# Finch attention and Fourier mixing on one core: GpSimd ordered behind VectorE's planned port operations, with several forms per chunk and a new order

## Chip, cores and metric

The kernel runs on 1 core of one Trainium2 chip. The metric is device time in microseconds (us) of one execution, and several executions are measured. Engines are named as the profile names them: PE is TensorE, DVE is VectorE, ACT is ScalarE, POOL is GpSimd, SP is SyncE.

## What is computed

```python
state = 0                                   # per batch and head, 48 x 48
for t in range(768):                        # r, k, v, w: 4 batches x 8 heads x 768 x 48
    cur = (u * k_t) outer v_t
    y[t] = r_t @ (state + cur)
    state = w_t[:, None] * state + k_t outer v_t
x = y laid out as (4, 768, 384)
mixed = real(fft(fft(x, axis=1), axis=2))
u = x + mixed
un = (u - mean(u)) / sqrt(var(u) + 1e-6)    # over the 384 columns
out = u + relu(un @ w_ch1) @ w_ch2          # 384 -> 1536 -> 384
```

All inputs and the output are float32; the kernel multiplies on PE mostly in bf16.

## The kernel before

A helper class records operations and a table emits them. `_Prog.op` (lines 168 to 203) notes an operation with the engines that may do it, a planned duration for each, the tiles that it reads and writes, and the operations that it depends on. The table ORDER (lines 40 to 111) was found beforehand: for each of the five engines a list of operation numbers. `_Prog.schedule` (205 to 291) walks the lists with the planned durations, only to hand out the eight PSUM banks. `_Prog.emit` (303 to 395) then writes each engine's instructions in the order of its list, with semaphore waits where an operation depends on another engine's. So an engine takes its instructions strictly in the listed order, and a waiting instruction holds back all that stand behind it on that engine, or in SP's queue.

Some operations are marked as users of the SBUF port that DVE and POOL share (the argument `port`, and every POOL instruction that isn't a DMA). In the plan a marked operation starts only when the other engine's last marked one has ended. Nothing of this is emitted: on the chip no semaphore ties the two.

The work goes over 4 batches of 768 tokens, each in 6 chunks of 128 tokens (24 chunks, numbered n). For a chunk, `load` (288 to 306) brings w, k, r and v, 192 KB each, from seven rotating buffers of each kind, all on SP's queue. `attention` (728 to 883) then does, per chunk:

- the log of w on ACT (742), two matmuls that sum logs over the chunk (744, 748) and exponentials of them (750, 763)
- the bonus: products r*k and r*k*u (767, 769), a reduction per head on DVE (771, `dc`), and `vtd = v*dc` (774)
- `vb`, v in bf16 (777, on ACT or DVE); `rh = r*exp` (782, DVE, out of PSUM); `kh = k*exp` (785, DVE or POOL)
- the transposes of rh and kh: on PE, a bank for each, evicted by ACT or DVE (794 to 808), or for batch 3 (n >= 18) by one DMA on SP's queue (790)
- scores on PE (814), two masked copies on DVE (819), the state's update (844 to 856)
- y on PE (864 to 875), to which the bonus vtd is added: in chunks 0 to 4 of batch 0 by an fp32 matmul with the identity that opens the bank (860), then an eviction (877), elsewhere by DVE's add (879).

`fold` (885 to 913) forms sums and differences of mirrored columns, and from batch 1 on of chunks c and c+3 (`sd`, then `xf`). `mix` (915 to 1058) does the Fourier sums along the sequence (936 to 939) and the columns (963), adds x (968 in batch 0, 979 in the others), takes mean and variance (985), normalises (`un`, 971 or 987), transposes un on PE (998, batches 0 and 1) or by DMA (1004, batches 2 and 3), and goes through the feed-forward: 12 first groups of three matmuls for each half batch (1027), a relu on ACT or DVE (1032), and for each row of 128 tokens three groups of four matmuls (1046), the last add on DVE (1052) and an output DMA on SP's queue (1056). `weights` (713 to 723) brings both weight matrices by three DMAs from POOL's queue, W1 in two halves and W2 in one. 32 matmuls without a use (1101) stand in PE's list as fillers, and 16 at the start (1069).

`mix` of one batch is interleaved with `attention` of the next in all five lists. Helpers record many operations under one line: 537 is every two-input product or sum that DVE or POOL may do, 541 and 542 operations with scalars, 551 and 560 ACT's and 561 DVE's copies.

Of the kernel before, what the change touches and what calls it, by code (L numbers as in the profile page):

```python
# [22 lines left out]
DMA_T, DMA_U, T_RK, T_UN, T_XFER, T_LAT = 18, 2, 1240, 1280, 1500, (1250, 450)  # L23
# [11 lines left out]
YPE = (0, 1, 2, 3, 4)  # L35

# [30 lines left out]
    "act": (  # L67
# [13 lines left out]
    "dve": (  # L81
# [45 lines left out]
class _Op:  # L127
    def __init__(self, alts):
# [10 lines left out]
        self.start = None  # L139
        self.end = None  # L140
        self.inc = False
        self.ready0 = 0


class _Prog:
# [59 lines left out]
    def schedule(self, order):  # L205
# [18 lines left out]
        for left in range(len(self.ops)):  # L224
# [35 lines left out]
            if o.port:  # L260
                port[e] = s + o.dur
# [873 lines left out]
```

## Time and profile before

| | |
|---|---|
| three runs | 193.33, 192.1, 189.92 us; median 192.1 |
| profiled execution | span 188.1 us from the first to the last instruction; its own time is not given beside the span |
| granted TensorE clock | 1.000 |
| DMA | 28.99 MB, 154 GB/s over the span |
| HBM | 23.59 MB read, 4.72 MB written |
| POOL: products rk<-in_r,in_k | 21 of 1033 ns |
| DVE: masked copies (819) | 48 of 678 ns |
| ACT: relu (1035) | 71 of 492 ns |

The table of groups gives for each line, engine and pair of tiles the count, the time busy, the mean of one, and the idle time of the engine just ahead of them with what ended it. Busy times of matmuls overlap, so a busy PE isn't a PE at its peak. In the chain that ended last each piece was released by the one ahead of it; "SPq" there is SP's queue, in which only DMA issues stand. A view of a stretch of time gives for each engine its busy time there, with the number of instructions in brackets.

### The profile page before, as it was taken

Reading aid. Unit: us, or ns where it says so; the run is one execution under the profiler, and the core shown is the slowest. Engines: PE = TensorE matmul, PEld = TensorE weight load, DVE = VectorE, ACT = ScalarE, POOL = GpSimd, SP = SyncE. Lnnn points to the kernel's source line nnn. Section 1 sums busy time; section 2 is a strip of 40 time slices with the busy share of each in tenths; the row PEclk is TensorE's granted clock in tenths of the full one; section 3 lists DMA queues with packets and bytes.
Section 4 is the critical chain, followed back from the end, with each engine's and each line's share of the span. In section 5 each row is a group of like instructions: output and inputs, shape, how many; then the busy total and the mean of one; then the engine's idle time right before and its main releaser. Section 6 shows DMA issues by size and latency. Waiting matters only on the chain.

```text
span 188.1 us, 4561 instructions
## 1 busy us (share of the span) xinstructions
PE 176.4 (94%) x1718; PEld 115.1 (61%) x1718; DVE 161.0 (86%) x359; ACT 125.4 (67%) x297; POOL 107.1 (57%) x127
## 2 busy tenths in 40 slices
PE   5998899589999989999999997999999999999994
PEld 2565576356656657776667664766666666666663
DVE  8899998999997999999999997899999879732233
ACT  2898696469795967799898769884763373447300
POOL 3558899992052927679999887699774200000000
PEclk9999999999999999999999999999999999999999
DMA  6999899999999508989999999977752110630043
GB/s 122 224 203 204 179 204 209 187 200 198 206 182 195 104 0 185 244 171 209 199 216 227 217 140 273 216 142 176 135 97 67 45 42 8 141 105 0 0 167 125
DMA packets 116118, 28.99 MB, mean 154 GB/s; under 512 B 111361, under 2 KB 116098, under 8 KB 116098
## 3 DMA queue, kind: packets, MB, share of 16 engines
q1 hardware_dynamic: 114514, 26.36, 68.0%
q0 software_dynamic: 1584, 2.36, 7.1%
q8 instruction: 13, 0.21, 0.4%
q14 instruction: 7, 0.06, 0.1%
HBM read 23.59 MB, written 4.72 MB: 150 GB/s over the span
## 4 chain that ended last, share of the span: by engine, by line
PE 51%; DVE 19%; POOL 10%; SPq 7%; DMA 5%; issue 4%; ACT 3%; DVEq 0%; ACTq 0%; POOLq 0%
PE bank L1027 19%; PE bank L1046 17%; POOL rk L537 5%; SPq L583 5%; PE bank L963 5%; DVE rkh L537 3%; DMA in_w<-in_w_dram 3%; DVE ah L819 3%; DMA in_k<-in_k_dram 3%; PE bank L939 2%; POOL rkh L537 2%; DVE rkh L782 2%; PE bank L814 2%; DVE rk L537 1%; POOL vtd L537 1%
## 5 line engine op out<-in xcount | busy, mean ns | idle before, releaser
L1027 PE MATMUL bank<-unt,w 128*128 128x384 bf16 x288 | 53.3, 326 | 1.0 <-ACT ht L1035 0.9
L1046 PE MATMUL bank<-w,ht 128*128 128x384 bf16 (+2 forms) x300 | 53.6, 319 | 0.0
L1035 ACT ACTIVATE ht<-bank 128x384 bf16<-128x384 f32 x71 | 32.5, 492 | 14.8 <-PE bank L1027 14.7
L1027 PEld LDWEIGHTS bank<-unt,w 128*128 128x128 bf16 x288 | 26.6, 98 | 17.4 <-ACT ht L1035 1.1
L1046 PEld LDWEIGHTS bank<-w,ht 128*128 128x128 bf16 x300 | 27.6, 97 | 15.6
L819 DVE TENSOR_TENSOR ah<-bank,msk 128x512 bf16<-128x512 f32 x48 | 31.0, 678 | 0.5 <-PE bank L814 0.5
L537 POOL TENSOR_TENSOR rk<-in_r,in_k 128x384 f32<-128x384 f32 x21 | 21.6, 1033 | 9.7 <-DVE dc L771 9.0
L1052 DVE SCALAR_TENSOR_TENSOR osb<-bank,rstd,uf 128x384 f32<-128x384 f32 (+2 forms) x25 | 14.9, 596 | 11.1 <-PE bank L1046 10.6
L537 POOL TENSOR_TENSOR rkh<-in_k,e 128x384 bf16<-128x384 f32 x17 | 17.0, 1002 | 12.1 <-ACT e L763 10.4
L537 POOL TENSOR_TENSOR rk<-rk,ub 128x384 f32<-128x384 f32 x21 | 21.1, 1014 | 2.4 <-DVE rk L537 1.2
L537 POOL TENSOR_TENSOR vtd<-in_v,dc 128x384 f32<-128x384 f32 x22 | 18.7, 856 | 2.7 <-DVE dc L771 1.6
L560 ACT ACTIVATE rkt<-bank 128x512 bf16<-128x512 bf16 x30 | 17.2, 595 | 3.2 <-PE bank L804 1.9
L1033 DVE TENSOR_SCALAR ht<-bank 128x384 bf16<-128x384 f32 x25 | 13.0, 547 | 5.5 <-PE bank L1027 5.5
L537 POOL TENSOR_TENSOR xf<-sd 128x384 bf16<-128x384 f32 (+1 forms) x11 | 11.8, 1084 | 8.0 <-DVE sd L537 7.8
L551 ACT ACTIVATE un<-uf,agg 128x384 bf16<-128x384 f32 x19 | 11.2, 621 | 6.3 <-DVE agg L985 5.3
L551 ACT ACTIVATE lb<-in_w 128x384 bf16<-128x384 f32 x24 | 12.2, 523 | 3.6 <-DMA in_w<-in_w_dram 3.4
L763 ACT ACTIVATE e<-bank 128x392 f32<-128x392 f32 (+1 forms) x24 | 11.7, 496 | 4.0 <-DVE bank L848 1.7
L782 DVE TENSOR_TENSOR rkh<-bank,in_r 128x384 bf16<-128x384 f32 x24 | 13.1, 548 | 0.7 <-ACT bank L750 0.7
L750 ACT ACTIVATE bank<-bank 128x384 f32<-128x384 f32 x24 | 11.6, 488 | 2.5 <-PE bank L744 2.3
L771 DVE TENSOR_REDUCE dc<-rk 128x8 f32<-128x384 f32 x24 | 12.9, 538 | 0.1
L551 ACT ACTIVATE vb<-in_v 128x384 bf16<-128x384 f32 x22 | 11.5, 524 | 0.8 <-DMA in_v<-in_v_dram 0.8
L870 PE MATMUL bank<-vb,ah 128*128 128x48 bf16 x192 | 11.1, 183 | 0.0
(147 smaller groups left out, 353.8 us busy)
## 6 DMA issues: line engine op xcount, KB each, us to landing
in_k<-in_k_dram SPq DMA_DIRECT2D x24, 192.0 KB, 3.7
in_w<-in_w_dram SPq DMA_DIRECT2D x24, 192.0 KB, 3.9
in_v<-in_v_dram SPq DMA_DIRECT2D x24, 192.0 KB, 3.8
in_r<-in_r_dram SPq DMA_DIRECT2D x24, 192.0 KB, 3.9
out_dram<-osb SPq DMA_DIRECT2D x23, 192.0 KB, 2.2
w<-in_moe_w_ch_dram POOLq DMA_DIRECT2D x2, 576.0 KB, 8.5
w<-in_moe_w_ch_dram POOLq DMA_DIRECT2D x1, 1152.0 KB, 15.5
out_dram<-osb SPq DMA_DIRECT2D x1, 128.0 KB, 1.7
```

Source lines behind the costliest of these rows:

```text
L537: return lambda e: e.tensor_tensor(out=o, in0=a, in1=b, op=f)
L551: return lambda e: e.activation(o, a, f, **kw)
L560: {"act": lambda e: e.activation(o(), i(), ACTF.Copy), "dve": lambda e: e.tensor_copy(out=o(), in_=i())}, **kw)
L763: op("act", a_ps(ne), lambda e: e.activation(E2[i2][:, 0:ne], ps(tci)[:, 0:ne], ACTF.Exp), r=[tci], w=[("E2", i2)])
L771: op("dve", v_1(DM), lambda e: e.tensor_reduce(out=dc[:, :], in_=rku[:, :, :], axis=mybir.AxisListType.X, op=ALU.add), r=[("RK", i2)], w=[ ...
L782: op("dve", v_1(DM), lambda e: e.tensor_tensor(out=rh[:, :, 0:D], in0=ps(tce)[:, 0:DM].rearrange("t (h d) -> t h d", d=D), in1=rt[:, :, :] ...
L819: masked[n] = op("dve", v_1(512), lambda e, x=x: e.tensor_tensor(out=ah[:, x:H:2, :], in0=ps(ta[x])[:, :].rearrange("p (h t) -> p h t", t= ...
L1027: ins = e.matmul(ps(t)[:, 0:384], W1[:, m, 256 * (j // 2) + j % 2:256 * (j // 2) + 256:2], unt[:, :, m, :], start=(m == 0), stop=(m == NM ...
L1033: {"dve": lambda e, j=j, t=t, ht=ht: e.tensor_scalar(out=ht[:, j, :], in0=ps(t)[:, 0:384], scalar1=su, scalar2=0.0, op0=ALU.mult, op1=ALU. ...
L1035: "act": lambda e, j=j, t=t, ht=ht: e.activation(ht[:, j, :], ps(t)[:, 0:384], ACTF.Relu, scale=su)},
L1046: ins = e.matmul(ps(t)[:, 0:hi - lo], ht[:, j, 128 * x:128 * x + 128], W2[:, j, lo:hi], start=(j == 0), stop=(j == NJ - 1))
L1052: op("dve", v_1(hi - lo) + 64, lambda e, kb=kb, t=t, o=o, lo=lo, hi=hi: e.scalar_tensor_tensor(out=o[:, lo:hi], in0=ps(t)[:, 0:hi - lo], s ...
```

## The change

Four things are done.

1. POOL waits. In `schedule` each marked POOL operation, its DMAs now included, gets a dependency on the last marked DVE operation that the plan starts ahead of it, so `emit` writes a semaphore wait for it. The plan has DVE wait for POOL as before, and nothing is emitted for that.
2. Forms. A new method `choose` records several ways of doing a step, and the lists name the operations of one of them; the others are dropped. The forms are: rh out of PSUM, or through a row in SBUF (`rh_row`); transposes over two banks, over one bank with one eviction of 1024, or by DMA; the mask in one DVE operation, or as an ACT copy and a product on DVE or POOL; y plus bonus out of PSUM, through a row, or by the fp32 matmul that opens the bank (batch 0); the normalised rows' transposes on PE or by DMA; the adds to u and to the output out of PSUM or through a row. `vb` may also be made on POOL.
3. What the new lists choose. Bonus by fp32 matmul: chunks 1 and 3 of batch 0 (5 chunks before). Transposes: one bank for 8 chunks, two banks for 10, DMA for batch 3's six as before. rh through a row: 2 chunks. Masks in two steps: 4 of 48 (two products on DVE, two on POOL). y through a row: 1 chunk; u through a row: 3 rows. Transposes of un: PE for batch 0 and the first half of batch 1, DMA for the rest (27 on PE against 36, 5 DMAs against 4). `vb`: 17 on ACT, 5 on POOL, 2 on DVE. The fillers stay 32.
4. The lists themselves are new on all five engines. Batches and stages lie much as before. On DVE the last rows of batch 0's feed-forward come in the order kb = 1, 2, 0, 5, 4, 3 (before 1, 0, 2, 5, 4, 3). On SP the first output (kb = 2) still stands behind the load of w for batch 2's chunk 1. The 2 later weight DMAs wait for DVE operations: W1's second half for the last of DVE's products of batch 1 that stand behind batch 0's folds, W2 for the first `un` on DVE. POOL's instructions that wait for DVE are 45 (31 before), DVE's that wait for POOL 44 (35).

```diff
-            alts[e] = (d, fn[e] if isinstance(fn, dict) else fn, (e == "pool" and sem is None) or e in port)
+            alts[e] = (d, fn[e] if isinstance(fn, dict) else fn, e == "pool" or e in port)
...
+    def choose(self, name, *ways):
+        wr0, rd0, left = self.wr, self.rd, []
+        for v, way in enumerate(ways):
+            self.wr = {x: list(y) for x, y in wr0.items()}
+            self.rd = {x: list(y) for x, y in rd0.items()}
+            self.cho = (name, v)
+            way()
+            left.append((self.wr, self.rd))
...
     def schedule(self, order):
+        kept = {o for e in self.ENGS for o in self.order[e]}
+        self.ops = [o for o in self.ops if o in kept]
...
                 if o.port:
-                    p = port["pool" if e == "dve" else "dve"]
-                    late = int(e == "dve" or p <= s)
-                    s = max(s, p)
+                    late = int(e == "dve" or port["dve"] <= s)
+                    s = max(s, port["pool"] if e == "dve" else last.end + self.LAT["pool"] if last else 0)
...
             if o.port:
                 port[e] = s + o.dur
+                if e == "dve":
+                    last = o
+                elif last:
+                    o.deps.add(last)
...
+        def rh_row():
+            op("act", a_ps(DM), lambda e: e.activation(e1[...], ps(tce)[:, 0:DM], ACTF.Exp), ...)
+            vec(DM, tt(rh[:, :, 0:D], rt[:, :, :], e1[:, :, :], ALU.mult), ...)
+        g.choose(("rh", b, c), rh_bank, rh_row)
...
-        op(None, {"act": a_sb(DM), "dve": v_2(DM)},
+        op(None, {"act": a_sb(DM), "dve": v_2(DM), "pool": 560},
...
-        if n >= DMA_T:
+        def tr_one():
+            t = g.tile("a")
+            for x, (rows, name) in enumerate(((rflat, "RH"), (kflat, "KH"))):
...
+            evict(lambda: RKT[i4][:, :, :].rearrange("p h t -> p (h t)"), lambda: psb(t)[:, 0:1024], 1024, 2, ...)
+        g.choose(("tr", b, c), *([tr_two, tr_one, tr_dma] if b else [tr_two, tr_one]))
...
+            def twice(x=x, msk=msk, bk=bk):
+                op("act", a_ps(512), lambda e: e.activation(ah[:, x:H:2, :], ps(bk)[...], ACTF.Copy), ...)
+                masked[n].append(op(None, {"dve": v_2(512), "pool": p_1(512)},
+                                    tt(ah[:, x:H:2, :], ah[:, x:H:2, :], msk, ALU.mult), port=("dve",), ...))
+            g.choose(("mask", b, c, x), once, twice)
...
-        ype = b == 0 and c in YPE
+        g.choose(("x", b, c), add_bank, add_row, *([add_pe] if b == 0 else []))
...
-            if b < DMA_U:
+                g.choose(("un", b, hf), un_pe, un_dma)
```

More of the change, by code (lines that the diff above doesn't have):

```diff
@@ L163, in __init__ @@
         self.count = {}
+        self.cho = None
+    def choose(self, name, *ways):
[6 more added lines that the diff above has]
+            left.append((self.wr, self.rd))
+        self.cho = None
+        self.wr, self.rd = {}, {}
+        for wr, rd in left:
+            for had, has in ((wr, self.wr), (rd, self.rd)):
+                for x, y in had.items():
+                    z = has.setdefault(x, [])
+                    z += [o for o in y if o not in z]
     def tile(self, pool):
@@ L206, in schedule @@
         self.order = {e: [self.ops[int(i)] for i in order[e].split()] for e in self.ENGS}
+        kept = {o for e in self.ENGS for o in self.order[e]}
+        assert all(o in kept or o.cho for o in self.ops)
+        self.ops = [o for o in self.ops if o in kept]
+        for o in self.ops:
+            o.deps &= kept
+            for t in o.tile:
+                t.ops = [x for x in t.ops if x in kept]
         at = {e: 0 for e in self.ENGS}
@@ L209, in schedule @@
         port = {"dve": 0, "pool": 0}
+        last = None
         bank = [None] * 8
@@ L278, in schedule @@
                 o.end = self._land(max(t, s + o.set), o.xfer, sw) + o.post
+                if len(hw) >= 4:
+                    engt[e] = max(engt[e], sum(h[2].end - h[2].post for h in hw[-4:-2]) // 2)
             else:
@@ L472, in bass_rwkv6_finch__then__fnet_fourier_mix_kernel @@
     RSTD = [sb("rstd%d" % i, [NC], FP32) for i in range(2)]
-    UN = [sb("un%d" % i, [3, DM], BF16) for i in range(2 if DMA_U < B else 1)]
+    UN = [sb("un%d" % i, [3, DM], BF16) for i in range(2)]
     UNT = [sb("unt%d" % i, [3, NM, 128], BF16) for i in range(2)]
@@ L818, in attention, with once @@
         for x in range(2):
[L819 to L822 removed]
+            masked[n] = []
+            msk = MSK[:, :].unsqueeze(1).to_broadcast([128, HP, 128])
+            bk = ta[x]
+            def once(x=x, msk=msk, bk=bk):
+                masked[n].append(op("dve", v_1(512), lambda e: e.tensor_tensor(
+                    out=ah[:, x:H:2, :], in0=ps(bk)[:, :].rearrange("p (h t) -> p h t", t=128), in1=msk, op=ALU.mult),
+                    r=[bk, "MSK"], w=[("AH", i2, x)]))
+            def twice(x=x, msk=msk, bk=bk):
+                op("act", a_ps(512), lambda e: e.activation(
+                    ah[:, x:H:2, :], ps(bk)[:, :].rearrange("p (h t) -> p h t", t=128), ACTF.Copy), r=[bk], w=[("AH", i2, x)])
+                masked[n].append(op(None, {"dve": v_2(512), "pool": p_1(512)},
+                                    tt(ah[:, x:H:2, :], ah[:, x:H:2, :], msk, ALU.mult), port=("dve",), r=["MSK"], w=[("AH", i2, x)]))
+            g.choose(("mask", b, c, x), once, twice)
         ty = g.tile("a")
@@ L856, in attention, with ymat @@
                 op("dve", v_1(DM), lambda e: decay(e, s_flat), r=[tds, ("E2", i2)], w=[("ST", c % 2)])
[L858 to L864 removed]
+        def ymat(e, ype=False):
             for q in range(HP):
@@ L872, in ymat, with yop, add_bank, add_row @@
             return ins
-        op("pe", mm(D, 8) + (0 if first else mm(96, 4)), ymat,
-           r=[("AH", i2, 0), ("AH", i2, 1), ("VB", n % 4)]
-           + ([] if first else [("RTB", i4), ("ST", (c + 1) % 2)]), w=[ty])
-        if ype:
-            evict(lambda: xb[:, c, 0:DM], lambda: ps(ty)[:, 0:DM], DM, r=[ty], w=[("X", b % 2, c)])
-        else:
-            op("dve", v_1(DM), lambda e: e.tensor_tensor(
-                out=xb[:, c, 0:DM], in0=ps(ty)[:, 0:DM],
-                in1=vtd[:, :, :].rearrange("t h d -> t (h d)"), op=ALU.add),
-               r=[ty, ("VTD", n % 4)], w=[("X", b % 2, c)])
+        def yop(f):
+            op("pe", mm(D, 8) + (0 if first else mm(96, 4)), f, r=[("AH", i2, 0), ("AH", i2, 1), ("VB", n % 4)]
+               + ([] if first else [("RTB", i4), ("ST", (c + 1) % 2)]), w=[ty])
+        vflat = vtd[:, :, :].rearrange("t h d -> t (h d)")
+        def add_bank():
+            yop(ymat)
+            op("dve", v_1(DM), lambda e: e.tensor_tensor(out=xb[:, c, 0:DM], in0=ps(ty)[:, 0:DM], in1=vflat, op=ALU.add),
+               r=[ty, ("VTD", n % 4)], w=[("X", b % 2, c)])
+        def add_row():
+            yop(ymat)
+            op("act", a_ps(DM), lambda e: e.activation(xb[:, c, 0:DM], ps(ty)[:, 0:DM], ACTF.Copy), r=[ty], w=[("X", b % 2, c)])
+            vec(DM, tt(xb[:, c, 0:DM], xb[:, c, 0:DM], vflat, ALU.add), r=[("VTD", n % 4)], w=[("X", b % 2, c)])
+        def add_pe():
+            op("pe", mm(DM, 4), lambda e: e.matmul(ps(ty)[:, 0:DM], IDF[:, :], vflat, start=True, stop=False, skip_group_check=True),
+               r=["IDF", ("HT", 0, 0), ("VTD", n % 4)], w=[ty])
+            yop(lambda e: ymat(e, True))
+            evict(lambda: xb[:, c, 0:DM], lambda: ps(ty)[:, 0:DM], DM, r=[ty], w=[("X", b % 2, c)])
+        g.choose(("x", b, c), add_bank, add_row, *([add_pe] if b == 0 else []))
         fold(b, c)
```

125 lines of the change are left out of this document (72 added, 53 removed), and 132 rows, old and new, of the table ORDER.

## Prediction

> **What bounds the kernel now.** I read the page's head and its engine shares first, then busy time by stage, then the chain that ended last.
>
> ```profile
> span 188.1 us, 4561 instructions
> ...
> PE 176.4 (94%) x1718; PEld 115.1 (61%) x1718; DVE 161.0 (86%) x359; ACT 125.4 (67%) x297; POOL 107.1 (57%) x127
> ...
> PE 51%; DVE 19%; POOL 10%; SPq 7%; DMA 5%; issue 4%; ACT 3%; DVEq 0%; ACTq 0%; POOLq 0%
> ```
>
> ```profile
> core 0: us, PE busy (x) PEld busy (x) DVE busy (x) ACT busy (x) POOL busy (x), PEclk, DMA share, GB/s
> 0.00:45.00 45.00, 37.82 (x405) 24.20 (x406) 42.21 (x107) 32.19 (x68) 34.13 (x50) 1.00 1.02 193
> 45.00:60.00 15.00, 15.00 (x123) 9.34 (x122) 14.14 (x33) 10.51 (x28) 2.81 (x4) 1.00 1.02 194
> 60.00:70.00 10.00, 9.20 (x114) 6.00 (x113) 9.85 (x18) 8.27 (x22) 6.30 (x7) 1.00 0.37 73
> 70.00:110.00 40.00, 39.91 (x472) 27.78 (x470) 39.55 (x85) 34.49 (x83) 34.58 (x38) 1.00 0.98 206
> 110.00:120.00 10.00, 8.91 (x94) 5.89 (x92) 8.26 (x17) 7.70 (x22) 7.59 (x8) 1.00 1.15 207
> 120.00:158.30 38.30, 38.30 (x346) 24.94 (x345) 34.93 (x79) 22.39 (x56) 21.65 (x24) 1.00 0.47 100
> 158.30:188.20 29.90, 27.30 (x180) 16.96 (x178) 12.02 (x26) 9.85 (x25) 0.00 (x0) 1.00 0.30 86
> ```
>
> Three stages show. Up to 45 us VectorE (DVE) is busy 42.2 of 45 and PE idles 7.2 us: batch 0's attention and folding, paced by DVE. From 45 us PE is busy nearly all the time, except 0.8 us at 60 to 70 and 1.1 us at 110 to 120. After 158.3 only feed-forward matmuls are left, and 2.6 us of run-out. So after 45 us a gain must come out of PE's own work or out of those two holes; before 45 us it must come out of DVE.
>
> The chain, in order of time, says the same:
>
> ```profile
> 39.11 1.27 DVE rkh L537
> ...
> 45.01 2.06 PE bank L1027 x12
> ...
> 55.94 1.30 PE bank L1046 x8
> ...
> 69.79 0.54 DVE osb L1052
> 70.35 0.37 SPq L1056
> ...
> 107.50 5.52 DMA in_w<-in_w_dram
> ...
> 114.50 1.15 PE bank L1027 x6
> ```
>
> The first feed-forward matmul (L1027) starts at 45.0. The hole at 110 to 120 goes back through a late load to SyncE's queue (SPq), which at 70.35 had been released by DVE's third output row.
>
> **The change, part by part.**
>
> *GpSimd (POOL) waits for the DVE operation that the plan puts ahead of it.* These are groups of DVE operations with their shortest, median and longest time (the third, fed from PSUM, never varies), and below them one meeting with POOL in full (POOL first, then DVE):
>
> ```profile
> L537 DVE TENSOR_TENSOR xf<-x x4: 342/1044/1802, 31.5 to 37.5; 128x192 bf16<-128x192 f32 x2, 128x191 bf16<-128x191 f32 x2
> L537 DVE TENSOR_TENSOR rkh<-in_k,e x7: 550/1178/1351, 15.4 to 107.3; 128x384 bf16<-128x384 f32 x7
> L782 DVE TENSOR_TENSOR rkh<-bank,in_r x24: 537/546/558, 10.3 to 136.2; 128x384 bf16<-128x384 f32 x24
> L541 DVE TENSOR_SCALAR ss<-ss,sgs x1: 1383/1383/1383, 7.3 to 7.3; 128x285 bf16<-128x285 bf16 x1
> ```
>
> ```profile
> 33.23 0.61 POOL L537 TENSOR_TENSOR xf<-x 128x191 bf16<-128x191 f32 x1
> 33.77 0.78 POOL L716 DMA_DIRECT2D w<-in_moe_w_ch_dram  x1
> 34.54 0.86 POOL L720 DMA_DIRECT2D w<-in_moe_w_ch_dram  x1
> 35.42 1.00 POOL L537 TENSOR_TENSOR rkh<-in_k,e 128x384 bf16<-128x384 f32 x1
> ```
>
> ```profile
> 33.18 3.47 DVE L537 TENSOR_TENSOR xf<-x 128x192 bf16<-128x192 f32 x2
> ```
>
> Two folds that take 0.34 us each when free took 3.47 us while POOL ran a fold, two weight DMAs and a product without a break: 3.47 - 2 x 0.34 = 2.8 us lost. The products rkh<-in_k,e, 0.55 us when free, lose about 1.18 - 0.55 = 0.6 each; some four of the seven fall before 45 us, 2.2 to 2.5 us. The table mirror ss is single; its free price has no row, between 0.34 (the short folds') and 1.38, so it lost 0 to 1.0, say 0.5. Before 45 us that is 2.8 + 2.2 + 0.5 = 5.5 us on the engine that paces the stage. At 64 us two more meet:
>
> ```profile
> 63.88 1.30 DVE L537 TENSOR_TENSOR rk<-rk,ub 128x384 f32<-128x384 f32 x1
> 65.11 1.18 DVE L537 TENSOR_TENSOR rkh<-in_k,e 128x384 bf16<-128x384 f32 x1
> ```
>
> Another 1.4 us, ahead of the output row at 69.7.
>
> The new waits put DVE's folds (now in one run with the products of batch 1) ahead of POOL's products and of the second weight DMA. In batch 2 DVE is given no marked operation between its last fold of batch 1 and the first of batch 3, so POOL's long chain there meets no new wait. What is queued behind a wait is POOL's next products, and behind these DVE's reduction. The nearest row to a late partner is one free operation, 0.55 us per wait; with a dozen distinct DVE operations waited for, between 0 and 6.6 us of POOL time, on an engine 57% busy. I take a third of the 5.5 us as given back: net **-3.6 us** up to 45 us; ends 0 and -5.5.
>
> The row says that DVE lost 2.8 us behind POOL. [...]
>
> *Weight DMAs moved.* The plan now counts them as port users. The first stays ahead of the folds; the second follows the fold cluster; the third (W2) waits for DVE's first normalised row, after first-L1027.
>
> ```profile
> DMA to landing us min/median/max: 7.6/9.4/15.5
> ```
>
> The shortest, 7.6 us, is a half-size one with nothing ahead; the 15.5 us is W2 behind two. W2 alone therefore lands between 7.6 us and 15.5 us after its issue; doubling the half's 7.6 as to data gives 11, which I take. It leaves about 1.4 us after the first L1027 (one DVE row and a mask later), so it lands 9.0 to 16.9 after it, 12.4 likeliest. L1046 needs all of it: now 55.94 - 45.01 = 10.9 us later, with 19 groups ahead; the new order puts 21 groups and attention steps ahead, some 12.5 us. Cover is then zero: cost 0 likeliest, 4.4 at the end; I take **+0.5**.
>
> *Bonus on PE in 2 chunks of batch 0 instead of 5; transposes of the normalised rows of batch 1's second half by DMA; masks, copies, exponentials in other forms.*
>
> ```profile
> 20.73 0.70 PE bank L860 x2
> ...
> 43.37 0.17 PE bank L998 x3
> ```
>
> ```profile
> 139.06 1.30 SPq L1004 DMA_TRANSPOSE unt<-un  x1
> ```
>
> ```profile
> L819 DVE TENSOR_TENSOR ah<-bank,msk 128x512 bf16<-128x512 f32 x48 | 31.0, 678 | 0.5 <-PE bank L814 0.5
> L560 ACT ACTIVATE rkt<-bank 128x512 bf16<-128x512 bf16 x30 | 17.2, 595 | 3.2 <-PE bank L804 1.9 <-PE bank L798 1.1
> L879 DVE TENSOR_TENSOR x<-bank,vtd 128x384 f32<-128x384 f32 x19 | 10.2, 548 | 0.5 <-POOL xf L537 0.5
> L561 DVE COPY rkt<-bank 128x512 bf16<-128x512 bf16 x6 | 2.5, 416 | 0.0
> ```
>
> Three fp32 matmuls fewer are 3 x 0.70 = 2.1 us of PE, but before 45 us, where PE idles 7.2 us: worth nothing by itself, and DVE gets three adds (3 x 0.55 = 1.6 us) for it; one mask fewer and four evictions and a bonus copy moved to ACT (0.68 + 4 x 0.42 + 0.42) pay 2.8 back there; two or three more products on DVE take about as much again. Zero. Three rows of transposes (3 x 0.17 = 0.5 us) leave a saturated PE: **-0.5**, and SyncE issues one more transpose, 1.30 us, ahead of an output and of batch 3's loads from chunk 1's k on: bounds -0.5 and, if these come late by that, +1.3. Four masks of 48 go over ACT: DVE loses 4 x 0.68, gets two SBUF products, between 0.34 and 0.68 each. Eight pairs of transposes are evicted in one 1024-wide copy: between one 512 (0.60) and two (1.19), so ACT's load is between -4.8 and 0 there; against it stand 13 evictions and exponentials more, some 5 us on an engine 67% busy. Over the kernel DVE's free work stays within 1 us: about 18 operations more of 0.55 on it, and masks, 512-copies and PSUM adds fewer. All zero, covered by PE after 45 us.
>
> *The queue of loads.*
>
> ```profile
> 60.18 1.12 SPq L583 DMA_DIRECT2D in_w<-in_w_dram  x1
> 70.35 0.37 SPq L1056 DMA_DIRECT2D out_dram<-osb  x1
> ```
>
> Nothing is issued for 9 us, because the first output stands ahead of batch 2's loads and its row (kb=2) is the third that DVE makes, sixteen operations after the first. In the new order it is the second, five after the first: eleven operations of 0.55, 6 us; and the 1.4 us of meetings may go. Batch 2's loads go out some 6 us nearer to the first output row; so the hole at 110 to 120 (1.1 us) should close at least half: **-0.6**, bounds 0 and -1.1.
>
> **Sum:** -3.6 + 0.5 - 0.5 - 0.6 = -4.2, so 188.1 becomes 183.9 us of span. The profile gives only the span of its execution, 4.0 below the median 192.1 of the runs; with the same 4.0 around it, the forecast is **187.9 us**, 2.2% less. What a measurement of this kernel tells from no change is about 2%, 3.8 us.
>
> **Rivals.**
> 1. *Port time is conserved.* POOL, 34.1 of 45 us busy up to the first L1027, gets later by what DVE gains, and DVE waits for its products. For it: DVE has more waits on POOL in the new order. Against: DVE's operations fed from PSUM meet nothing (537 to 558 ns in all 24 of rkh<-bank), so the plan can run POOL beside them. Then only -0.5 - 0.6: 191.0. It also stands for a change that does not do what it says, the order being set already.
> 2. *W2 lands late.* If landing takes 15.5 us even with nothing ahead, PE stops 4.4 us at the first L1046 and attention of batch 1 behind it. That eats the gain: 187.9 + 3.9 = 191.8; with rival 1 as well, 195.
> 3. *A POOL wait takes the lead: slower.* Place: the folds of batch 1 and what follows, 70 to 110 us, where POOL is busy 34.6 of 40 us and DVE 39.6. All of POOL's products of batch 2 stand behind DVE's last fold of batch 1. If the two engines come to wait for each other in turn, each of the dozen waits costs a POOL instruction (1.00, the row at 35.42) on top of the work: 12 us, between 6.6 and 12 x 1.55 = 18.6. POOL's 5.4 us of slack there cover the first; from there on it goes into the loads that need POOL's buffers and into PE: 12 - 5.4 = 6.6, giving 187.9 + 6.6 = 194.5, ends 189 and 201. It passes the time of before when more than 5.4 + 4.2 = 9.6 us are lost. Against it: in batch 2 itself there is no new wait.
> 4. *All meetings vanish and both holes close:* -5.5 - 0.5 - 1.9: 184.2.
>
> **How the numbers follow.** Forecast 0.40; conserved 0.20; W2 late 0.10; POOL wait 0.18; all vanish 0.12. The likeliest has a range of its own of 186 to 190.5. The range, 183.8 to 194.5, takes in every case but half of the POOL wait, the sum of rivals 1 and 2, and a better end than rival 4. Faster by over 2% is below 188.3: 0.12, six tenths of 0.40, and 0.04 of the others, 0.40. Slower by over 2% is above 195.9: not quite half of the POOL wait, 0.08, and 0.05 of W2 late together with conserved port time: 0.13. The rest, 0.47, is within 2%.
>
> **What would show it.** Right: DVE's folds and products near their shortest times (0.34, 0.55); the first L1027-form matmul at 41 to 42 us; SyncE's gap ahead of the first output 5 us or less; PE busy to the end from there. Wrong: DVE idle with POOL as releaser before the first L1027; PE waiting for the w DMA at the first L1046; a new late load.

## Result, and the profile after

The changed kernel takes 184.96 us, median of four executions (184.76 to 190.94), against 191.83 us (189.92 to 193.33) of the kernel before: ratio 0.9662, 95% interval 0.9584 to 0.9741. The forecast was 187.9 with a range of 183.8 to 194.5. The profiled execution took 184.91 us with a span of 183.0, so 1.9 us lie around the span. Single executions of several kernels came out 2 to 4% longer than the rest of theirs (the 190.94 here); ratios leave these out, and so they leave out part of the kernel before too, whose executions scatter most (188.15 to 194.49 in the group that was measured most often).

The page of the changed kernel, its head and its chain by engine:

```profile
span 183.0 us, 4506 instructions
...
PE 173.6 (95%) x1703; PEld 113.9 (62%) x1703; DVE 154.8 (85%) x358; ACT 127.9 (70%) x296; POOL 102.6 (56%) x126
...
PE 66%; DMA 11%; ACT 9%; DVE 8%; POOL 2%; issue 2%; SPq 0%; DVEq 0%; ACTq 0%
```

The chain has moved from DVE (19%, now 8) and POOL (10%, now 2) to PE (51%, now 66). DVE works 6.2 us less and POOL 4.5 us less, with nearly the same number of instructions. The same stretches of time as before the change:

```profile
core 0: us, PE busy (x) PEld busy (x) DVE busy (x) ACT busy (x) POOL busy (x), PEclk, DMA share, GB/s
0.00:45.00 45.00, 40.76 (x431) 26.31 (x432) 39.76 (x115) 37.23 (x76) 28.52 (x45) 1.00 0.98 187
45.00:60.00 15.00, 13.02 (x128) 8.33 (x126) 11.65 (x27) 11.02 (x31) 4.18 (x6) 1.00 1.01 179
60.00:70.00 10.00, 10.00 (x117) 6.72 (x115) 9.96 (x20) 8.20 (x19) 7.17 (x9) 1.00 1.03 208
70.00:110.00 40.00, 40.00 (x461) 27.73 (x459) 38.86 (x84) 35.45 (x85) 34.58 (x38) 1.00 0.99 202
110.00:120.00 10.00, 9.67 (x109) 6.79 (x108) 9.45 (x21) 9.13 (x24) 6.69 (x7) 1.00 1.05 202
```

Both holes of PE are nearly closed (9.20 to 10.00 at 60 to 70, 8.91 to 9.67 at 110 to 120). A new one of 2.0 us stands between 45 and 60. Groups of DVE operations, with shortest, median and longest time:

```profile
L571 DVE TENSOR_TENSOR xf<-x x4: 349/350/352, 32.5 to 33.9; 128x191 bf16<-128x191 f32 x3, 128x192 bf16<-128x192 f32 x1
L571 DVE TENSOR_TENSOR rkh<-in_k,e x10: 540/551/559, 9.2 to 104.5; 128x384 bf16<-128x384 f32 x10
L571 DVE TENSOR_TENSOR xf<-sd x11: 546/549/554, 76.5 to 144.6; 128x384 bf16<-128x384 f32 x6, 128x382 bf16<-128x382 f32 x5
L571 DVE TENSOR_TENSOR rk<-rk,ub x4: 548/554/769, 8.3 to 131.1; 128x384 f32<-128x384 f32 x4
```

No fold and no product rkh takes more than its free time now. The table of who waits for whom (total, times, longest) shows POOL now waiting behind DVE, and what the new hole is:

```profile
POOL vtd L571 <- DVE rkh L571: 6.3, 2, 5.7
...
POOL xf L571 <- DVE xf L571: 4.8, 2, 3.4
...
POOL rk L571 <- DVE rk L571: 3.5, 2, 1.9
...
PE bank L1128 <- DMA w<-in_moe_w_ch_dram: 2.0, 1, 2.0
```

The chain in order of time, around that hole and at batch 2's late load:

```profile
40.38 2.94 POOL rk L571 x3
43.32 11.62 DMA w<-in_moe_w_ch_dram
55.08 0.81 PE bank L1128 x4
...
103.13 4.07 DMA in_v<-in_v_dram
107.22 0.52 ACT vb L585
```

W2's load is issued at 43.32, when three products ahead of it on POOL are done, and lands 11.6 us later; PE waits 2.0 us for it. SP's queue at the first output, where it had stood idle for 9 us, goes on without a gap:

```profile
61.66 2.02 SPq L617 DMA_DIRECT2D in_w<-in_w_dram  x2
63.72 1.59 SPq L1148 DMA_DIRECT2D out_dram<-osb  x1
```

Below are the starts of the first first-group matmul of each batch (line 1027 or 1109, read off the timelines), in the profiled execution of each kernel. The distances between neighbours say in which stage time is gained. They are single executions, and a few tenths of a us are nothing.

| kernel | batch 0 | batch 1 | batch 2 | batch 3 | end of span |
|---|---|---|---|---|---|
| before | 44.9 | 89.9 | 131.0 | 162.0 | 188.1 |
| changed | 40.4 | 85.9 | 126.4 | 156.8 | 183.0 |
| new order, no waits | 42.2 | 87.3 | 129.4 | 161.4 | 187.5 |
| old order, with waits | 42.1 | 86.1 | 127.9 | 158.9 | 185.1 |
| old order, waits, output later | 42.1 | 86.0 | 127.1 | 158.1 | 184.2 |
| changed, W2's load early | 41.1 | 84.9 | 126.2 | 156.8 | 183.0 |
| waits up to W2's load only | 40.1 | 85.6 | 127.6 | 159.2 | 185.4 |
| waits behind W2's load only | 41.1 | 84.5 | 124.8 | 155.4 | 181.6 |
| waits in batch 1 only | 41.1 | 84.5 | 126.2 | 158.3 | 184.5 |
| waits in batches 2 and 3 only | 42.9 | 88.0 | 129.5 | 160.1 | 186.2 |

4.5 us of the 5.1 are there at the first group, and the stages behind it give -0.5 (45.0 became 45.5), 0.6, 0.6 and about 0. The stage that became longer holds PE's 2.0 us of waiting for W2.

### The profile page after: what moved, and what is told of

The parts are those of the page before. It is cut to its first block, busy times and chain, and to the rows that moved or that the text cites. A ratio compares the mean times of both kernels' runs of the same rounds, so it can differ in the third digit from the quotient of the medians.

```text
span 183.0 us, 4506 instructions
## 1 busy us (share of the span) xinstructions
PE 173.6 (95%) x1703; PEld 113.9 (62%) x1703; DVE 154.8 (85%) x358; ACT 127.9 (70%) x296; POOL 102.6 (56%) x126
## 4 chain that ended last, share of the span: by engine, by line
PE 66%; DMA 11%; ACT 9%; DVE 8%; POOL 2%; issue 2%; SPq 0%; DVEq 0%; ACTq 0%
PE bank L1128 23%; PE bank L1109 17%; DMA w<-in_moe_w_ch_dram 6%; DMA in_v<-in_v_dram 5%; PE bank L1034 5%; PE bank L1010 4%; PE bank L868 3%; DVE ah L878 2%; ACT ht L1117 2%; ACT e L810 2%; PE bank L845 2%; POOL rk L571 2%; PE bank L905 2%; PE bank L1193 1%; PE bank L782 1%
## 5 line engine op out<-in xcount | busy, mean ns | idle before, releaser
L1109 PE MATMUL bank<-unt,w 128*128 128x384 bf16 x288 | 51.6, 326 | 0.2 <-DVE x L940 0.2
L878 DVE TENSOR_TENSOR ah<-bank,msk 128x512 bf16<-128x512 f32 x44 | 28.6, 681 | 1.9 <-PE bank L868 1.7
L571 POOL TENSOR_TENSOR rk<-rk,ub 128x384 f32<-128x384 f32 x20 | 20.0, 1008 | 7.2 <-DVE rk L571 3.5
L594 ACT ACTIVATE rkt<-bank 128x512 bf16<-128x512 bf16 (+1 forms) x25 | 17.8, 718 | 3.1 <-PE bank L845 1.5
L571 POOL TENSOR_TENSOR rk<-in_r,in_k 128x384 f32<-128x384 f32 x17 | 16.9, 1004 | 0.9 <-DVE ht L1115 0.9
L571 POOL TENSOR_TENSOR rkh<-in_k,e 128x384 bf16<-128x384 f32 x14 | 14.1, 1005 | 2.3 <-ACT un L585 1.5
L585 ACT ACTIVATE un<-uf,agg 128x384 bf16<-128x384 f32 x21 | 12.3, 617 | 3.0 <-DVE agg L1062 2.9
L788 DVE TENSOR_TENSOR rkh<-bank,in_r 128x384 bf16<-128x384 f32 x22 | 12.0, 548 | 0.7 <-ACT bank L787 0.5
L940 DVE TENSOR_TENSOR x<-bank,vtd 128x384 f32<-128x384 f32 x21 | 11.6, 551 | 1.2 <-PE bank L929 0.5
L929 PEld LDWEIGHTS bank<-vb,ah 128*128 128x128 bf16 x192 | 9.5, 96 | 2.0 <-DVE ah L878 0.6
## 6 DMA issues: line engine op xcount, KB each, us to landing
w<-in_moe_w_ch_dram POOLq DMA_DIRECT2D x1, 1152.0 KB, 11.6
```

What stands on the lines that cost most here:

```text
L571: return lambda e: e.tensor_tensor(out=o, in0=a, in1=b, op=f)
L585: return lambda e: e.activation(o, a, f, **kw)
L594: {"act": lambda e: e.activation(o(), i(), ACTF.Copy), "dve": lambda e: e.tensor_copy(out=o(), in_=i())}, **kw)
L878: masked[n].append(op("dve", v_1(512), lambda e: e.tensor_tensor(out=ah[:, x:H:2, :], in0=ps(bk)[:, :].rearrange("p (h t) -> p h t", t=128 ...
L929: ins = e.matmul(ps(ty)[:, D * h:D * h + D], ah[:, h, :], vb[:, h, :], start=first and not ype, stop=True, skip_group_check=True)
L1109: ins = e.matmul(ps(t)[:, 0:384], W1[:, m, 256 * (j // 2) + j % 2:256 * (j // 2) + 256:2], unt[:, :, m, :], start=(m == 0), stop=(m == NM ...
```

## Experiments

The theory on trial is the prediction's: the emitted waits take away DVE's meetings with POOL up to the first group, and that is the gain. The rival is that the new order does it. The kernels ran in three groups, each on one chip; where two kernels of different groups are compared, the table's distances carry the reading, and the medians only beside them. Where lists are edited, the PSUM banks were held as the unedited lists give them.

**The new order without waits.**

```diff
-                elif last:
-                    o.deps.add(last)
```

> The new orders on all five engines, without the semaphore waits of GpSimd on VectorE's planned port operations. Theory (the waits hold the order that the plan chose; without them GpSimd, when it is early, gets in front of VectorE's folds and products): DVE's folds xf<-x rise again from 0.35 us and rkh<-in_k,e from 0.55, two or more us before the first feed-forward matmul, which moves from 40.4 to 42 to 44 us; time 186.5 to 189. Rival (the new order alone does it, the waits never hold anything): groups as in the new kernel, first feed-forward matmul at 40.4, time 185.

188.84 us, ratio 0.9918 (0.9867 to 0.9969); of the 5.1 us of span 0.6 are left. So the waits are needed. But the groups show something else than the theory, which put the loss ahead of the first group:

```profile
L571 DVE TENSOR_TENSOR xf<-x x4: 348/350/351, 34.5 to 35.9; 128x191 bf16<-128x191 f32 x3, 128x192 bf16<-128x192 f32 x1
...
L571 DVE TENSOR_TENSOR rkh<-in_k,e x10: 542/551/1202, 9.8 to 105.9; 128x384 bf16<-128x384 f32 x10
L571 DVE TENSOR_TENSOR xf<-sd x11: 540/545/1351, 77.1 to 148.5; 128x384 bf16<-128x384 f32 x6, 128x382 bf16<-128x382 f32 x5
```

Batch 0's folds, which had lost 2.8 us, are free with no wait at all. POOL there, then DVE:

```profile
33.97 1.75 POOL L750 DMA_DIRECT2D w<-in_moe_w_ch_dram  x2
```

```profile
34.52 0.35 DVE L571 TENSOR_TENSOR xf<-x 128x192 bf16<-128x192 f32 x1
34.79 0.55 DVE L571 TENSOR_TENSOR rkh<-in_k,e 128x384 bf16<-128x384 f32 x1
35.26 0.35 DVE L571 TENSOR_TENSOR xf<-x 128x191 bf16<-128x191 f32 x1
```

The new order has no product of POOL beside them, only the two weight DMAs, and a weight DMA costs these two folds and the product nothing. Two DVE operations do meet POOL ahead of the first group, at 10.75 (1.29 us for a free 0.54) and 27.22 (0.93 for 0.54), and neither stands in the chain that ended last. Most of what comes back stands later, and in that chain:

```profile
68.37 1.56 DVE sd L571 x2
...
77.60 1.36 DVE xf L571
...
110.81 2.46 DVE sd L571 x2
...
134.90 1.27 DVE vtd L571
...
148.13 1.75 DVE xf L571 x2
```

Eight operations of a free 0.55 us take 8.40 us there: 8.40 - 8 x 0.55 = 4.0 us, all behind the first group. In the six of them that took 1.18 us or more, POOL's operation had started 0.24 to 0.43 us before DVE's. The page gives DVE 161.4 us busy and POOL 105.3 without the waits, 154.8 and 102.6 with them.

**The old order with waits.** The plan of the kernel before is kept, and each marked POOL operation gets a dependency on the marked DVE operation planned ahead of it.

```diff
             if o.port:
-                port[e] = s + o.dur
+                port[e] = s + o.dur; last, o.deps = (o, o.deps) if e == "dve" else (last, o.deps | {last} - {None})
```

> The old orders and forms, with the waits alone: each of GpSimd's port operations, its weight DMAs included, waits for the last port operation of VectorE that the old plan starts ahead of it. Theory (the meetings in the first 45 us are what the change takes away, and the old plan already meant them not to happen): xf<-x falls to 0.35 us, rkh<-in_k,e to 0.55 to 0.7, first feed-forward matmul at 41 to 43 instead of 45.0, SyncE's gap ahead of the first output shorter; time 186.5 to 189. Rival (the old plan did not mean the waits, so they move the loss to GpSimd): GpSimd idle behind DVE by 3 us or more before 45 us, first feed-forward matmul at 44 to 46, time 190 to 194.

187.06 us, ratio 0.9841 (0.9712 to 0.9970).

```profile
L537 DVE TENSOR_TENSOR xf<-x x4: 346/520/733, 31.3 to 34.6; 128x192 bf16<-128x192 f32 x2, 128x191 bf16<-128x191 f32 x2
...
L537 DVE TENSOR_TENSOR rkh<-in_k,e x7: 546/551/808, 16.1 to 103.8; 128x384 bf16<-128x384 f32 x7
```

Here the waits do in the main what the prediction said: the folds fall from 1044 ns in the median to 520 (not yet to a free 346), the products from 1178 to 551, and the first group comes at 42.1. So order and waits each bring the first group forward by some 2.7 us when alone, and by 4.5 together. They overlap, since both take away meetings there; how much of the new order's 2.7 it would have had at full clock is taken up below.

**W2's load right behind the second weight load, waits kept.** In POOL's list:

```diff
-338 570 616 527 611 528 339 631
+338 339 570 616 527 611 528 631
```

> The new kernel with the third weight DMA (W2) moved in GpSimd's queue from behind five products to right behind the second weight DMA; nothing else differs. It should be issued at about 36 us instead of 43.3 and land by 51. Theory (PE is the bound from 40 us on, so the 2.0 us that PE waits for W2 at the first L1128 are worth 2.0 us): that wait is gone, time 182.5 to 183.5. Rival (loads, at DMA share 1.0 until 113 us, set batch 3's pace, so what PE gains at 53 us it waits for later): wait gone, but batch 3's last loads land at the same time and PE idles at 105 to 120 instead; time 184.3 to 185.

185.79 us (184.75 to 186.65, and one of 189.28), ratio 0.9739 (0.9580 to 0.9899). PE no longer waits for W2. Batch 1's first group comes 1.0 us earlier, those of batches 2 and 3 at 126.2 and 156.8, where they were. The 2.0 us of the new hole are worth nothing at the end: the theory's 182.5 to 183.5 is out. Of the stage from batch 1 to batch 2, 40.5 us became 41.3; batch 0's first group came 0.7 us later, 0.4 of it PE's wait for W1's first half, behind a stretch at half clock that is taken up below.

**The old order, the first output four loads later in SP's list.**

```diff
-375 794 767 766 823
+794 767 766 823 375
```

> The old kernel with one move: in SyncE's queue the first output stands behind four more loads (w of batch 2's chunks 1 and 2, r and k of its chunk 0) instead of ahead of them. Theory (the 9 us without a load issue at 61 to 70 us is what makes the load late that PE waits for at 114): the gap shrinks by four loads, the wait of ACT and PE at 113 goes, time 0.5 to 1.5 us less than before. Rival (the loads after 70 us wait for buffers, not for the queue): loads after it land as before, time as before within 0.3 us.

188.07 us, ratio 0.9858 (0.9679 to 1.0037): unclear, and the profiled execution had TensorE at 0.79 of its clock at 36 to 44 us, so its stages can't be compared. It was tried again on top of the waits, below.

**Waits only up to W2's load, and only behind it.** The 41 first operations of POOL's list, or the rest:

```diff
-                elif last:
+                elif last and at[e] <= 41:
```

> The new kernel with the emitted waits only on GpSimd's first 41 operations, up to and with the W2 load (batch 0 and the first products of batch 1); behind these none. Theory (two separate losses without waits, 1.8 us before the first feed-forward matmul and 2.7 after it): first feed-forward matmul at 40.4 as in the new kernel, the later loss stays, time 187 to 188. Rival (the early waits do it all, what comes later follows from the early delay): time 184.8 to 185.5.

188.16 us, ratio 0.9849 (0.9782 to 0.9916), as the theory had it.

```diff
-                elif last:
+                elif last and at[e] > 41:
```

> The new kernel with the emitted waits only on GpSimd's operations behind the W2 load; on the first 41 none. Theory (two separate losses): PE's clock falls to half for some us between 8 and 18 us and the first feed-forward matmul comes at 42 as in the run without waits, but the later meetings are gone, time 186 to 187. Rival (the early waits do it all): time 188.5 to 189.5 as without any wait.

184.01 us (183.52 to 185.01), ratio 0.9618 (0.9562 to 0.9673), less than either expectation. Both ran on one chip, so this is the cleanest pair: with the early waits alone the kernel stays 0.7 us from the one without any; with the late ones alone it is as fast as the changed kernel, or 1 us faster, which the two intervals don't tell apart. The prediction's place for the gain, up to 45 us, is refuted as far as the waits go: the late waits are worth 4.2 us more than the early ones (188.16 - 184.01).

The traces show what the late waits take away. Count for each DVE operation what it took beyond the shortest of its kind (same operation, tiles and shape), where that is over 0.1 us. Behind the first group this comes to 6.8 us without waits and 6.5 with the early ones alone, and to 0.8 with the late ones alone and 1.0 with all.

In the table the stage from batch 0 to batch 1 is 45.5 us both with the early waits alone and with all. With all, W2's load is issued at 43.32 for 42.05, and PE waits 2.0 us for it where it waited 0.3; that hides there what the late waits save. With late waits alone PE doesn't wait for W2.

What still differs at the first group (40.1 and 40.4 in two kernels with the early waits, 41.1 to 42.9 in the new order without) is not DVE's meetings with POOL alone. In the stretches of 8 to 12 and 12 to 16 us, the changed kernel:

```profile
8.00:12.00 4.00, 3.46 (x38) 2.30 (x39) 3.13 (x9) 3.31 (x8) 1.80 (x4) 1.00 1.04 202
12.00:16.00 4.00, 3.60 (x55) 2.28 (x53) 3.18 (x7) 4.00 (x9) 3.87 (x5) 1.00 1.06 212
```

no waits:

```profile
8.00:12.00 4.00, 2.90 (x31) 2.24 (x31) 3.06 (x11) 2.86 (x7) 0.99 (x1) 0.74 1.04 207
12.00:16.00 4.00, 4.00 (x27) 2.20 (x26) 2.00 (x7) 2.96 (x6) 2.78 (x3) 0.50 0.95 183
```

waits behind W2's load only:

```profile
8.00:12.00 4.00, 3.45 (x31) 2.64 (x31) 2.95 (x13) 2.96 (x7) 0.95 (x1) 0.60 1.07 210
12.00:16.00 4.00, 3.60 (x42) 2.04 (x39) 2.33 (x7) 3.71 (x7) 2.96 (x4) 0.97 1.07 211
```

The number behind POOL's is the granted TensorE clock. In the profiled executions of the new order without early waits, and in both with them and an early W2, it falls to half for 3.4 or 6.8 us (summed over stretches of 1 us). Where that lasts through 12 to 16 us, PE does 27 to 29 matmuls there for 55. The three kernels of that kind reach the first group at 41.9 to 42.9, the four with a dip at 8 to 12 only at 41.1, the two without any at 40.1 and 40.4. The clock isn't the whole of it: with W2's load early, and with waits in batches 2 and 3 only, PE also waits 0.4 us for W1's first half. But the kernel without batch 0's outputs has no such wait and, by the same count as above, no meeting ahead of the first group, and with 6.8 us at half clock it comes 1.5 us later than the changed one. Since kernels with the early waits have it too, they are no sure way round it. Over all executions, though, none of the 39 of the new order without early waits kept its full clock (a mean of 0.999 or more over the span), and 6 of the 16 with them did.

The executions' times go with it: 3.4 us at half clock are 1.7 of some 186 us, 0.009 in the mean clock, and the kernel with the waits in batch 1 only, further down, took 186.4 and 186.6 us at 0.991, 187.5 to 188.1 at 0.982 (and once 193.7), and 188.9 at 0.973. So it is fairer to compare kernels at one clock. At 0.990 or 0.991 there are, over several chips, two executions without waits (187.90 and 188.50), two with early waits (188.18 and 188.13), one with late waits (183.52) and one with all (184.76): there the early ones are worth nothing, and the late ones 4.7 us by themselves and 3.4 on top of the early ones.

**The old order with waits and the later output.** The edits of the second and the fourth experiment together.

> The old orders with both repairs: the waits, and the first output behind four more loads. With the waits alone the time was 187.06 and SyncE's gap ahead of the first output 4.1 us. Theory (the gap and the meetings are separate causes): the gap falls under 1 us, time 185.5 to 186.5, so that little is left for the new orders and forms (184.96). Rival (with the meetings gone the output row comes early enough): time 186.6 to 187.4, and the rest of the gain belongs to the new orders and forms.

185.59 us (185.28 to 186.52), ratio 0.9702 (0.9649 to 0.9755). The gap at the first output falls from 4.1 us to 1.3 and batch 2's first group comes 0.8 us earlier (127.1 against 127.9). The old lists with these two repairs stand 0.6 us above the changed kernel by the medians, 1.2 by the spans: forms and new order bring little beyond them, and by the ratios' intervals nothing certain.

**W2's load early, and batch 0's six output loads left out.** This kernel doesn't write batch 0's rows; its time is that of less work on SP's queue.

> The new kernel with the W2 load early, and without the six output DMAs of batch 0 (batch 0's rows are left out of the output): 1.2 MB and six places in SyncE's queue less between 63 and 95 us. The W2 load early alone did not change the time (first group of batch 1's feed-forward 1.0 us earlier, of batch 2's 0.2, of batch 3's 0.0). Theory (the loads, at a DMA share of 1.0 until 113 us, set the pace of batches 2 and 3): the last loads land 3 to 6 us earlier, batch 2's feed-forward starts 1 to 3 us earlier, time 182 to 184. Rival (loads are early enough, another engine paces batches 2 and 3): loads land earlier, feed-forward as before, time 184.5 to 185.

186.25 us over all four, 184.32 and 182.95 without the two long ones; ratio 0.9592 (0.9506 to 0.9677). The first groups stand at 41.9, 85.7, 125.8 and 156.2 us, the end of the span at 182.4. The last fourteen loads land 0.4 to 1.4 us earlier than with the outputs (3 to 6 were expected), and the distance from batch 1 to batch 2 is 40.1 us for 41.3; the others are the same within 0.2. So the load queue is a part of the pace behind batch 1, worth about 1.2 us in that stage.

**Late waits only, with W2's load early.**

> The changed kernel without the GpSimd waits ahead of W2's load, and with that load moved right behind the second weight load (the two edits that, one at a time, gave 184.01 and 185.79 us, the changed kernel being 184.96). Theory A (the early waits cost POOL up to 1 us and W2's late landing costs nothing at the end): 183.9 to 184.3 us, PE without its 2 us wait ahead of the first L1128 group, but the first L1109 groups of batches 2 and 3 where they were without the move (124.8 and 155.4 us). Theory B (both matter and add up): below 183 us, with batch 3's first L1109 group at or before 154 us. Theory C (the early waits matter for nothing, 184.01 was scatter): 184.9 us.

188.55 us over six: 185.41, 185.47 and 186.49, and three of 190.6 to 191.1, one of which was profiled; ratio of the short ones 0.9835 (0.9741 to 0.9930). None of the three theories fits, C with 184.9 is nearest: the kernel is no faster than with either edit alone. The profiled execution is one of the longest, so what it shows is not the price of the edit, but it can be followed. SP's queue, DVE and PE there, and the stretch with the granted clock behind POOL's number:

```profile
33.65 0.83 SPq L617 DMA_DIRECT2D in_v<-in_v_dram  x1
...
37.33 8.79 SPq L617 DMA_DIRECT2D in_r<-in_r_dram  x1
46.16 4.51 SPq L617 DMA_DIRECT2D in_k<-in_k_dram  x1
```

```profile
49.78 0.36 DVE L826 CAST vb<-in_v 128x384 bf16<-128x384 f32 x1 [3.56 <-DMA in_v<-in_v_dram]
```

```profile
50.46 1.78 PE L1109 MATMUL bank<-unt,w 128*128 128x384 bf16 x5 [3.15 <-DVE unt L595]
```

```profile
44.00:60.00 16.00, 12.85 (x93) 7.32 (x92) 8.67 (x22) 9.82 (x27) 4.29 (x6) 0.79 1.01 189
```

With three weight loads in a row (issued from 32.87 to 34.61), the issue of one load of r stands for 8.79 us. That stall isn't what DVE waits for: the load of v had been issued ahead of it, at 33.65, and landed at 49.76. DVE waits 3.56 us for it and PE 3.15 us behind DVE. Then PE's clock is at half for 6.8 us, from 49.5 on, 2.2 us into PE's pause. Batch 1's first group comes at 91.0, 6.5 us later than with late waits alone: 3.15 of it is the pause, and the half clock accounts for 2.9 at most, an estimate from half of the 5.8 us of it that are left when PE goes on. In the kernel before a load of k stood for 8.58 us (at 36.03), and in the one without batch 0's outputs a load of v for 8.75 (at 39.52); PE stood still for at most 0.2 us behind either, so such a stall need not cost anything. Whether the other long executions are long in the same way isn't shown, and the profiled one tells nothing of the three short ones, which are no faster than the changed kernel.

**Late waits, split.** POOL's twenty operations behind W2's load up to batch 1's folds, or those behind them:

```diff
-                elif last:
+                elif last and 41 < at[e] <= 61:
```

> The changed kernel with the GpSimd waits only for POOL's operations of batch 1 behind W2's load (twenty of them, ending with batch 1's folds). With no waits it took 188.84 us, with all waits behind W2's load 184.01. Distances between the first L1109 groups of batches 0, 1, 2, 3 and the end: without waits 45.1, 42.1, 32.0, 26.1 us; with the late waits 43.4, 40.3, 30.6, 26.2. Theory A (each stage pays for its own meetings): the first distance becomes 43.4, the others stay at 42.1 and 32.0; 187.1 us. Theory B (one stage decides, batch 1's folds, and the rest follows through the loads): 43.4, 40.3 and 30.6; 184 to 185 us. Theory C (batch 1's meetings are covered by PE): 188.8 us.

```diff
-                elif last:
+                elif last and at[e] > 61:
```

> The complement: the GpSimd waits only for POOL's operations behind batch 1's folds. Theory A (each stage pays for its own meetings): distances 45.1, 40.3, 30.6, 26.2 us, 185.7 us. Theory B (batch 1's folds decide and the rest follows): 45.1, 42.1, 32.0; 188.8 us. Theory C (only batches 2 and 3 count, batch 1's meetings are covered by PE): 184 us with distances 43.4 to 45.1 in the first stage made good later.

187.60 us (ratio 0.9932, 0.9870 to 0.9993) and 187.27 us (0.9908, 0.9854 to 0.9961); theory A's 187.1 is met by the first, its 185.7 not by the second. The distances between the first groups are what tells: with batch 1's waits 43.4, 41.7, 32.1; with those of batches 2 and 3 45.1, 41.5, 30.6; with both 43.4, 40.3, 30.6; with none 45.1, 42.1, 32.0. The first distance goes wholly with batch 1's waits and the third wholly with the later ones, as theory A had it; the second needs both. The meetings go the same way: of DVE's 6.8 us behind the first group the waits of batch 1 leave 4.7, and those of batches 2 and 3 leave 2.9. By the medians the halves bring 1.2 and 1.6 us of the 4.8 between no waits and late waits, over three chips; at a mean clock of 0.990 or 0.991 they bring 1.7 (two executions) and 2.3 (one) of 4.7. How the rest divides stays open.

## Why the prediction was right or wrong

The total was right within 3 us and the range held it; the argument under its main term did not hold.

1. *POOL's waits, -3.6 up to the first group.* Two thirds of 5.5 are 3.7, not 3.6, which changes nothing. Measured at that place: -4.5, inside the ends 0 and -5.5. The operations came to their free times as forecast (folds 0.35, products 0.55), and the first group at 40.4 for a forecast 41 to 42. The step that failed is the one that gave this to the waits. In the new order the folds are free without them, and for the end of the kernel the early waits are worth 0.7 us by the medians on top of no waits (nothing at equal clock), and nothing on top of the late ones. Its row was misread in one thing: the 3.47 us fold was put down to a fold, two weight DMAs and a product in a row, while two weight DMAs by themselves slow no fold in the new order. That the first of the two old folds waited through a DMA as well (1.75 us in all, behind a POOL fold of 0.61) is left open.
2. *"All zero, covered by PE after 45 us", and no new wait met in batch 2.* This is where the waits earn their time. DVE is without marked operations only up to 104.5 in the changed kernel's trace: batch 2's folds run on it at 107.8 to 113.8, and POOL waits 3.2 us for them there. The new order alone puts meetings of 4.0 us into the chain behind the first group, which the trace of before had only in small part (the 1.4 us at 64). The late waits remove them: 4.8 us where there were none (188.84 to 184.01), 3.2 on top of the early ones (188.16 to 184.96). I read the price of the meetings off the old order; a new order has its own, and those had no row yet. PE busy near 100% hid nothing: without waits PE is busy for 39.16 of the 40 us at 70 to 110, and the meetings of that stage stand in the chain all the same. I take it that what PE does at such a moment isn't what the chain waits for; no run tests that by itself.
3. *A third of the gain given back through POOL.* Not seen. POOL waits for DVE in many places (6.3, 4.8 and 3.5 us in the groups above) and no such wait stands in the chain. Without waits, both engines were busy longer, DVE by 6.6 and POOL by 2.7 us; here the waits took the loss from DVE, which stands in the chain, to POOL, which is busy for 56% of the span. In the trace without waits POOL had started first by 0.24 to 0.43 us in the six long meetings of the chain. The rival of 191.0, in which POOL gets later by what DVE gains, is refuted by the 3.2 to 4.8 us above.
4. *W2, +0.5.* The load was issued 2.9 us after the first group, not 1.4, and took 11.6 us, where 11 was taken. PE waited 2.0 us, between the ends 0 and 4.4, and the term was too small by 1.5. Yet taking that wait away changes nothing at batches 2 and 3, so as a share of the end it should have been about 0.
5. *The load queue, -0.6.* The gap of 9.1 us is gone, and the hole at 110 to 120 shrank from 1.1 to 0.3: 0.8 us, with other edits in the same run. In the old order the later output alone is worth 0.8 us in the profiles and 1.5 in the medians (187.06 and 185.59).
6. *Un-transposes by DMA, -0.5, and the other forms, 0.* Not tried one by one. Old lists with waits and a later output come within 0.6 us (1.2 by the spans) of all forms and the new order, so together they are worth about that.
7. *4.0 us around the span.* The executions that have both numbers show 1.9. Before's profiled execution was one of its lower ones, near 190.0, and not the median. With 1.9 the same sum gives 183.9 + 1.9 = 185.8, within 1 us of the measured time; that is luck in part, as the main term stood on the wrong operations and the shortfall behind the first group (points 2 and 4) was not in the sum. From span to span the change brings 5.1 us for a forecast 4.2; the ratio of the medians is larger because the kernel before scatters over 3.4 us and the changed one, but for its longest, over 0.3.

Of the rivals, conserved port time is refuted, W2 came late and did not count, POOL's wait took the lead nowhere (POOL has 34.58 us busy at 70 to 110, as before, and PE is busy for all of the 40), and the case in which all meetings vanish came nearest with 184.2, though by another sum.

## What to carry to other kernels

Ask of each group of waits by itself what it is worth, by leaving it out on the chip: here the early ones did nothing for the end, the late ones made the gain, and the profile of before pointed to the early ones. Without waits eight DVE operations in the chain took 8.40 us for a free 4.4; with them POOL waited for DVE up to 6.3 us in one group, and none of that stood in the chain. So order the meetings in favour of the engine in the chain and let the one with slack wait; check it in the chain of the new order, not in that of the old. A wait that PE shows is not yet a gain: the 2.0 us for W2 were taken away by an earlier load, and the end stayed where it was.

## What was not expected of the hardware

- The issue of a single 192 KB load on SP's queue took up to 8.79 us while weight loads of POOL's queue were in flight (8.75 and 8.58 in two other kernels), against a median of 0.8 us over all loads of the kernel before and 0.9 of the changed one.
- The granted TensorE clock fell to 0.50 within the first 17 us in several kernels, for 3.4 us (four of them) or 6.8 us (three), behind a pause of PE ahead of 8.6 us. The length of that pause doesn't decide: the changed kernel idled for 0.77 us and kept its clock, the one without batch 0's outputs idled for 0.39 and lost it. The longest of these pauses is 1.73 us; what tips the clock is left open.
- A weight DMA on POOL (two in 1.75 us, no waits) slowed neither folds (0.35 us each) nor a product (0.55) of DVE beside it. In the same run the operation `un` (TENSOR_SCALAR) took 0.75 us for a free 0.42 beside W2's DMA (at 43.46), and 0.73 in the same place with late waits alone.
- A DVE operation of 0.55 us took 1.36 in one meeting with a two-input operation of POOL (a fold, 1.18 us), and two in a row took 2.46 (no waits). The runs show these times; that a port which both engines share lies behind them is how the program marks its operations, and no run shows the port itself.
